# A sigmoid attention with two gated layers on one core: scores split in every batch, weights cut into 3 KB places, and a plan that is remade six times

## The chip, the core and the metric

The kernel runs on one core of a Trainium2 chip. Its engines are TensorE (PE), whose weight loads the trace shows apart as PEld, VectorE (DVE), ScalarE (ACT), GpSimd (POOL) and SyncE (SP). SP issues most of the DMAs and POOL the rest. The metric is the device time of one execution in microseconds (us), as the median of several runs.

## The reference

Three parts follow each other, all in float32:

```python
# attention: 4 batches, 12 heads, 448 tokens, head size 64
scores = q @ k^T / 8 - log(448)
x = sigmoid(scores) @ v                  # then [1792 tokens, 768]
# first layer, 768 -> 1536 -> 768
xn = x / sqrt(mean(x*x) + 1e-6) * rms_g
y = (silu(xn @ w_gate) * (xn @ w_val)) @ w_out
# second layer, 768 -> 2048 -> 768
h = y @ w_in
out = (h - tanh(h)) @ w_out2
```

## The kernel before

**Numbers in two parts.** A large product is made with three fp32r matmuls in place of one fp32 matmul. Each operand is cut into a high part (a cast to fp32r) and a low part (the value less its high part), and PE adds high·high, high·low and low·high. Each cut costs a cast on ACT or DVE and a subtraction on DVE. A call of `copy` records a cast, so all casts and copies have line 291. The subtractions have line 374 (weights), 730 and 785 (right-hand operands) and 579 (q and k).

**Attention.** A batch has six pairs of heads, and a pair lies on 128 partitions. For each pair the scores come in two halves of two 128-row pieces, ACT turns each piece into a sigmoid (line 623), and then the product with v follows (line 646). The scores of a pair are either whole fp32 matmuls (line 616) or split into three fp32r matmuls (line 596). `SPLIT_QK = (0, 1)` and `is_split` choose: pair (0, 0) and all of batches 2 and 3 are whole, the other 11 pairs are split. While attention runs, weights of the first layer are read, cut, and written back to DRAM, and from batch 2 on the right-hand operands of the first layer are made as well.

**The layers.** Batches go in two groups, (0, 1) and (2, 3). Each product uses seven block products in place of eight, whose sums and differences DVE makes. A job of a layer's first matrix (`seven_units`) has 63 matmuls (line 982), a set of its second matrix (`set_units`) 126 (line 925), and a set in the plain form (`block`) 144 (line 1007). Results of the second matrix are added up in DRAM by accumulating DMAs of POOL (line 799).

**Places.** `wt` has 8 places of 6 KB for each partition. Raw weights as they come from DRAM (`raw`), q and k of a pair (`qkr`), both parts of a job's weights (`op`), and both parts of a set's weight (`whl`, at most 3) share them. `cv` has 8 places of 3 KB, for values in float32, for weights that are read again (`again`, at most 4), and for v. `unit` has 72 places of 448 columns for all else.

**The plan.** The code records steps. `Plan.issue` then lays them out on five engine clocks with costs written in the code, and takes at each turn, of all that can start within `SOON = 300` of the soonest, the step with the lowest rank. A rank is the place in the recording plus a few offsets. The steps are then issued in order of their planned start. All engines run their own instructions in that order and wait on semaphores for each other.

Of the kernel before, what the change touches and what calls it, by code (L numbers as in the profile page):

```python
# [33 lines left out]
SPLIT_QK = (0, 1)  # L34
# [3 lines left out]
SOON = 300  # L38
# [11 lines left out]
N_UNIT, N_MOE, N_RAW, N_WT, N_CV = 72, 40, 2, 8, 8  # L50
# [21 lines left out]
class Plan:  # L72
# [21 lines left out]
    def issue(self):  # L94
        work, n_work = self.work, len(self.work)
# [12 lines left out]
        users = [[] for _ in work]  # L108
# [6 lines left out]
        slots = [list(dict.fromkeys(s for s, _ in (*w[2], *w[3]))) for w in work]  # L115
# [7 lines left out]
        free = {pool: [0.0] * size for pool, (size, _) in self.room.items()}  # L123
# [13 lines left out]
        issued = []  # L137
        frees = []
        import bisect
        import heapq  # L140

        def places(n):
# [13 lines left out]
            for k, x in want.items():  # L156
                if held[k] + x > cap[k]:
                    return None
                f = free[pool_of[k]]
                if len(f) < x:  # L160
                    return None
                t = max(t, f[x - 1])
            return t

        while len(issued) < n_work:
# [24 lines left out]
            if not cands:  # L190
                raise RuntimeError(f"no work can start; the oldest is {oldest}")
            soonest = min(c[1] for c in cands) + SOON
            finish, start, n, e, ns, uses_port = min((c for c in cands if c[1] <= soonest), key=lambda c: self.rank[c[2]])
# [3 lines left out]
            end[n], where[n], done[n] = finish + work[n][5], e, True  # L197
            waiting.remove(n)
            for s in slots[n]:
# [3 lines left out]
                if s.kind:  # L203
                    kind_at[s.kind] += 1
                    held[s.kind] += 1
                    since[s] = free[pool_of[s.kind]].pop(0)
            for s in slots[n]:
                left[s] = left.get(s, len(s.uses)) - 1
                if s.kind and not left[s]:
                    held[s.kind] -= 1  # L210
                    bisect.insort(free[pool_of[s.kind]], max(end[u] for u in s.uses) + self.OTHER)
# [6 lines left out]
            issued.append((start, n, e))  # L218
        for _, n, e in sorted(issued):
            for s in slots[n]:  # L220
                s.tile = s.tile or s.make()
            work[n][1](e)
        return max(clock.values())
# [3 lines left out]
def tile_sigmoid_attention_moe_moe(  # L227
# [20 lines left out]
    wt_p = ctx.enter_context(tc.tile_pool(name="wt", bufs=N_WT))  # L248
    cv_p = ctx.enter_context(tc.tile_pool(name="cv", bufs=N_CV))
# [5 lines left out]
        "unit": (N_UNIT, {"moe": N_MOE, "s": 18, "acc": 6, "accs": 9, "st": 4, "sum": 6, "x": 16, "xr": 4, "tmp_m": 8, "tmp_a": 4, "sq": 3, "rstd": 2,  # L255
                          "xs": 42, "tmp_s": 9, "tmp_x": 4, "qk": 12}),
        "wt": (N_WT, {"raw": N_RAW, "qkr": 4, "whl": 3, "op": 6}),
        "cv": (N_CV, {"cv": 3, "again": N_AGAIN, "vs": 3}),
# [10 lines left out]
    def unit(kind, dt=F32):  # L269
        return slot(kind, unit_p, [P, S], dt, "unit")  # L270

# [65 lines left out]
    def load_raw(src, by="SP"):  # L337
        flat = lambda t: t.bitcast(U16).rearrange("p n h -> p (n h)")
        r = slot("raw", wt_p, [P, NW + 1, 2], U32, "wt")
# [16 lines left out]
    def values32(r):  # L356


        c = slot("cv", cv_p, [P, NW], F32, "cv")
# [15 lines left out]

    def factors(j, names, of, reads):


        n = len(names)
        t = slot("op", wt_p, [P, 2, n, NH], F32R, "wt")  # L380
        w = lambda q: t.tile[:, q].rearrange("p n h -> p (n h)")
        hi, lo = (lambda: w(0), lambda: w(1)) if n == 2 else (
            lambda q=q: w(q).rearrange("p (k c) -> p k c", c=P) for q in range(2))
        split(n * NH, hi, lo, of, reads, [t["h"]], [t["l"]])
        use_factors(j, names, t)
        return t

    def use_factors(j, names, t):
        n = len(names)
        w = lambda q: t.tile[:, q].rearrange("p n h -> p (n h)")  # L390
        for x, name in enumerate(names):
            ops.setdefault(j, {})[name] = {p: (t, p, lambda k, x=x, q=q: w(q)[:, (k * n + x) * P:(k * n + x + 1) * P])
                                           for q, p in enumerate("hl")}
# [8 lines left out]
    def rows_early(ph, i):  # L402
# [15 lines left out]
        def total(to, x, y, at, sub=True):  # L418
# [3 lines left out]
            t = c[to] = c[at] if at else slot("cv", cv_p, [P, NW], F32, "cv")  # L422
# [26 lines left out]
    def pair_units(ph, i, rs, j):  # L449
# [8 lines left out]
        def sums():  # L458
            t = slot("cv", cv_p, [P, NW], F32, "cv")
# [15 lines left out]
        def keep(t, at, x):  # L475
            if (ph, i) not in SPLIT:
                put(d, at, x)
                return
            add({"SP": (2200, False)}, lambda e: nc.sync.dma_start(
                out=d.tile[:, at, :, :t.tile.shape[2] * NH], in_=t.tile.bitcast(F32).rearrange("p q n h -> p q (n h)")),  # L480
                [t["h"], t["l"]], [d[at]], after=LAND)
# [4 lines left out]
    def again(d, at):  # L486
        w = slot("again", cv_p, [P, NW], F32, "cv")
# [20 lines left out]
    def again_units(j):  # L508
        ph, _, i, _ = jobs[j]
        if (ph, i) in SPLIT:  # L510
            d = stored[ph, i]

            def load_parts(at, names):
                t = slot("op", wt_p, [P, 2, len(names), NH], F32R, "wt")
                add({"SP": (2200, False)}, lambda e: nc.sync.dma_start(
                    out=t.tile.bitcast(F32).rearrange("p q n h -> p q (n h)"), in_=d.tile[:, at, :, :len(names) * NH]), [d[at]], [t["h"], t["l"]], after=LAND)
                use_factors(j, names, t)
# [16 lines left out]
    def pair_load(b, p):  # L534
        t = qkr_t[b, p] = slot("qkr", wt_p, [P, 2 * S], F32, "wt")
# [703 lines left out]
```

## Time and profile before

| | |
|---|---|
| three runs | 1068.04 us median (1064.84, 1068.04, 1068.17) |
| the profiled execution | 1066.15 us |
| its span, first to last instruction | 1064.2 us |
| PE busy | 1042.9 us, 98% of the span |
| DVE, ACT, POOL busy | 789.2, 694.2, 141.8 us |
| moved by DMA | 245.65 MB, 231 GB/s |

The profiled execution has 2 us around its span. Matmuls overlap, so their mean duration (366 ns) says less than how far apart they start: a row such as 100 matmuls in 20.61 us does.

### The profile page before, as it was taken

Reading aid. Unit: us, or ns where it says so; the run is one execution under the profiler, and the core shown is the slowest. Engines: PE = TensorE matmul, PEld = TensorE weight load, DVE = VectorE, ACT = ScalarE, POOL = GpSimd, SP = SyncE. Lnnn points to the kernel's source line nnn. Section 1 sums busy time; section 2 is a strip of 40 time slices with the busy share of each in tenths; the row PEclk is TensorE's granted clock in tenths of the full one; section 3 lists DMA queues with packets and bytes.
Section 4 is the critical chain, followed back from the end, with each engine's and each line's share of the span. In section 5 each row is a group of like instructions: output and inputs, shape, how many; then the busy total and the mean of one; then the engine's idle time right before and its main releaser. Section 6 shows DMA issues by size and latency. Waiting matters only on the chain.

```text
span 1064.2 us, 15305 instructions
## 1 busy us (share of the span) xinstructions
PE 1042.9 (98%) x5236; PEld 880.7 (83%) x5236; DVE 789.2 (74%) x1252; ACT 694.2 (65%) x1251; POOL 141.8 (13%) x194
## 2 busy tenths in 40 slices
PE   8999999999999999999999999999999999999998
PEld 4553338999999889999998989989997899999997
DVE  3746985976877697866776668888885887777666
ACT  5776875675675566665675656777774767676752
POOL 1122001000003032101013030000303210003030
PEclk9999999999999999999999999999999999999999
DMA  6898886756759898778679399477949881839383
GB/s 202 265 309 270 252 302 219 289 179 230 274 178 244 318 258 235 266 266 322 238 247 281 116 249 304 173 253 275 240 154 258 236 241 51 282 104 236 96 192 130
DMA packets 105869, 245.65 MB, mean 231 GB/s; under 512 B 27072, under 2 KB 59328, under 8 KB 105792
## 3 DMA queue, kind: packets, MB, share of 16 engines
q1 hardware_dynamic: 82224, 179.63, 49.5%
q0 software_dynamic: 23264, 64.89, 24.8%
q8 instruction: 41, 0.67, 0.3%
q14 instruction: 36, 0.29, 0.1%
q10 hardware_dynamic: 304, 0.16, 0.1%
HBM read 151.44 MB, written 93.19 MB: 230 GB/s over the span
## 4 chain that ended last, share of the span: by engine, by line
PE 79%; issue 10%; DMA 5%; DVE 3%; POOL 2%; ACT 1%; SPq 0%; POOLq 0%; ACTq 0%; DVEq 0%
PE ps L982 39%; PE ps L925 21%; PE ps L646 7%; PE ps L1007 5%; PE ps L616 4%; PE ps L596 3%; POOL out L799 2%; DMA wt<-in_w_out 1%; DMA out<-unit 1%; DMA wt<-in_w_in 1%; DMA wt<-in_qkt 1%; DMA wAg<-cv 1%; DVE wt L374 1%; DVE unit L861 0%; DVE cv L363 0%
## 5 line engine op out<-in xcount | busy, mean ns | idle before, releaser
L982 PE MATMUL ps<-unit,wt 128*128 128x448 f32 x2520 | 522.4, 366 | 6.9 <-ACT unit L291 4.0
L982 PEld LDWEIGHTS ps<-unit,wt 128*128 128x128 f32 x2520 | 471.9, 188 | 51.0 <-ACT unit L291 6.6
L925 PE MATMUL ps<-unit,wt 128*128 128x448 f32 x1512 | 314.6, 366 | 3.5 <-DVE unit L730 1.6
L925 PEld LDWEIGHTS ps<-unit,wt 128*128 128x128 f32 x1512 | 283.4, 188 | 29.0 <-DVE unit L730 2.2
L374 DVE TENSOR_TENSOR wt<-cv,wt 128x768 fp32r<-128x768 f32 (+1 forms) x244 | 216.2, 892 | 91.1 <-ACT wt L291 88.3
L291 ACT COPY unit<-ps 128x448 f32<-128x448 f32 x297 | 156.3, 534 | 136.2 <-PE ps L982 53.6
L291 ACT CAST wt<-cv 128x768 fp32r<-128x768 f32 (+1 forms) x236 | 184.5, 786 | 81.5 <-PE ps L982 34.9
L730 DVE TENSOR_TENSOR unit<-unit 128x448 fp32r<-128x448 f32 x252 | 152.8, 620 | 36.7 <-ACT unit L291 22.1
L291 ACT CAST unit<-unit 128x448 fp32r<-128x448 f32 x259 | 143.0, 567 | 28.2 <-DVE unit L735 11.8
L861 DVE TENSOR_TENSOR unit<-ps,unit 128x448 f32<-128x448 f32 x168 | 103.4, 622 | 36.8 <-PE ps L982 19.8
L735 DVE TENSOR_TENSOR unit<-unit 128x448 f32<-128x448 f32 x144 | 87.6, 620 | 16.3 <-DMA unit<-sumB 8.9
L623 ACT ACTIVATE unit<-ps 128x448 f32<-128x448 f32 (+1 forms) x192 | 86.1, 549 | 7.3 <-PE ps L616 4.4
L646 PE MATMUL ps<-unit,cv 128*64 128x448 f32 (+1 forms) x384 | 77.5, 545 | 0.0
L799 POOL DMA_DIRECT2D sumB<-unit x48 | 41.4, 941 | 233.9 <-DVE unit L861 150.0
L363 DVE SCALAR_TENSOR_TENSOR cv<-wt,zero 128x768 uint32<-128x768 uint32 x68 | 64.8, 954 | 7.8 <-ACT zero L291 7.2
L291 ACT CAST zero<-wt 128x768 f16<-128x768 bf16 x52 | 56.0, 1076 | 11.5 <-DMA wt<-in_w_in 6.0
L1007 PE MATMUL ps<-unit,wt 128*128 128x448 f32 x288 | 60.6, 367 | 1.8 <-ACT unit L291 1.1
L646 PEld LDWEIGHTS ps<-unit,cv 128*64 128x64 f32 (+1 forms) x384 | 25.4, 136 | 44.5 <-issue 30.8
L1007 PEld LDWEIGHTS ps<-unit,wt 128*128 128x128 f32 x288 | 53.6, 188 | 7.9 <-ACT unit L291 1.8
L799 POOL DMA_DIRECT2D out<-unit x36 | 31.0, 949 | 181.6 <-DVE unit L861 165.0
L455 DVE TENSOR_TENSOR cv<-cv 128x384 f32<-128x384 f32 x80 | 42.8, 553 | 1.6 <-DMA wAg<-cv 1.0
L616 PE MATMUL ps<-wt 64*128 64x448 f32 (+1 forms) x208 | 42.7, 547 | 0.0
(49 smaller groups left out, 455.7 us busy)
## 6 DMA issues: line engine op xcount, KB each, us to landing
wt<-in_w_out POOLq DMA_DIRECT2D x28, 768.0 KB, 7.3
cv<-wD SPq DMA_DIRECT2D x56, 384.0 KB, 5.1
cv<-wB SPq DMA_DIRECT2D x36, 384.0 KB, 5.5
wt<-in_w_in SPq DMA_DIRECT2D x16, 768.0 KB, 5.9
sumB<-unit POOLq DMA_DIRECT2D x48, 224.0 KB, 8.3
wD<-cv POOLq DMA_DIRECT2D x28, 384.0 KB, 5.9
wt<-in_w_gate SPq DMA_DIRECT2D x12, 768.0 KB, 5.1
wt<-in_w_val SPq DMA_DIRECT2D x12, 768.0 KB, 5.5
```

The lines of the kernel that those rows point to most:

```text
L291: add(engines, lambda e: (nc.scalar.copy if e == "ACT" else nc.vector.tensor_copy)(to(), of()), reads, writes)
L374: add({**dve(n, psum=False), **pool(n)}, lambda e: ENG[e].tensor_sub(lo(), of(), hi().bitcast(F32)), [*reads, *kh], [*kl])
L616: nc.tensor.matmul(ps[i, c].tile[:n, :S], lhsT=t.tile[rows, at:at + n], rhs=t.tile[rows, :S], start=True, stop=True)
L623: add(act(S, psum=True), lambda e: nc.scalar.activation(to.tile[at:at + n, :S], ps.tile[:n, :S], AF.Sigmoid, bias=-math.log(S), scale=1.0 ...
L646: nc.tensor.matmul(ps.tile[i * D:(i + 1) * D, :S], lhsT=v.tile[:n, c, i, :], rhs=a[c][i].tile[:n, :], start=(c == 0), stop=(c == 3))
L730: add({**pool(S), **dve(S, psum=False)}, lambda e: ENG[e].tensor_sub(t["l"].tile, of.tile, t["h"].tile.bitcast(F32)), [of["t"], kh], [kl])
L735: add({**dve(S, psum=False), **pool(S)}, lambda e: ENG[e].tensor_sub(t.tile, x.tile, y.tile), [x["t"], y["t"]], [t["t"]])
L799: add({"POOL": (1100, False)}, lambda e: nc.gpsimd.dma_start(out=d.tile, in_=t.tile, accum_op=ALU.add), [t["t"], d["t"]], [d["t"]], after= ...
L861: add(dve(S), lambda e: nc.vector.tensor_add(t.tile, ps.tile[:, :S], t.tile), [ps["t"], t["t"]], [t["t"]])
L925: nc.tensor.matmul(ps.tile[:, :S], lhsT=part(a), rhs=x[b].tile, start=n in (1, 5) and kp == 0 and q == 0, stop=kp == n_kp - 1 and q == 2, ...
L982: nc.tensor.matmul(ps.tile[:, :S], lhsT=part(a), rhs=x[b].tile, start=n in ((1, 2, 5) if opening else (1, 5)) and i == 0 and q == 0, stop= ...
L1007: nc.tensor.matmul(ps.tile[:, :S], lhsT=wt, rhs=a[p].tile, start=start and i == 0, stop=stop and i == 2, skip_group_check=True)
```

## The change

- `SPLIT_QK` names all four batches and `WHOLE_QK = 2` leaves the first two pairs whole: 22 pairs are split in place of 11.
- The pool `wt` and the pool `cv` go. `raw` has its own two places of 6 KB; all else that was in them shares 20 places of 3 KB, called `part`. The high and low part of a weight, and q and k of a pair, are now two tiles each. At most 8 halves of `whl` (before: 3 whole ones), 8 of `op` (6 whole), 8 of `qkr` (4 whole) and 2 of `again` (4) are open at once. q and k are loaded by two DMAs in place of one, and the two parts of the jobs C 0 and C 1 are stored and loaded apart: SP issues 620 DMAs, 580 before.
- The plan is made up to six times. The first has the ranks of before; then `due` goes backward through the plan just made and gives each step the latest start that does not delay the end, and this is the rank of the next plan. The plan with the soonest modelled end is issued. `SOON` is 100.
- Caps of some kinds in `unit` grow (`accs` 12, `tmp_m` 10, `tmp_s` 12, `tmp_x` 6).

```diff
-SPLIT_QK = (0, 1)
+SPLIT_QK = (0, 1, 2, 3)
+WHOLE_QK = 2
-SOON = 300
+SOON = 100
-N_UNIT, N_MOE, N_RAW, N_WT, N_CV = 72, 40, 2, 8, 8
+PASSES = 6
+N_UNIT, N_MOE, N_RAW, N_PART = 72, 40, 2, 20
...
     def issue(self):
+        work, best, rank = self.work, None, self.rank
+        for _ in range(PASSES):
+            laid = self.lay(rank)
+            if laid is None:
+                break
+            times, freed = laid
+            ends = max(f for _, f, _ in times)
+            if best is None or ends < best[0]:
+                best = ends, times
+            rank = self.due(times, freed)
+        order = sorted((t[0], n, t[2]) for n, t in enumerate(best[1]))
...
+    def due(self, times, freed):
+        work = self.work
+        by_end = sorted(range(len(work)), key=lambda n: times[n][0])
+        end = max(f for _, f, e in times if e == "PE")
...
+        for n, us in freed.items():
+            then[n] += [(u, work[n][5] + self.OTHER) for u in us]
+        pe = [n for n in by_end if times[n][2] == "PE"]
+        for n, u in zip(pe, pe[1:]):
+            then[n].append((u, 0))
...
+            late[n] = min(-t, engine.get(e, -t)) - (f - s)
+            if e in ("PE", "DVE", "ACT"):
+                engine[e] = late[n]
...
-        "wt": (N_WT, {"raw": N_RAW, "qkr": 4, "whl": 3, "op": 6}),
-        "cv": (N_CV, {"cv": 3, "again": N_AGAIN, "vs": 3}),
+        "raw": (N_RAW, {"raw": N_RAW}),
+        "part": (N_PART, {"cv": 3, "again": 2, "vs": 3, "qkr": 8, "whl": 8, "op": 8}),
...
     def whole(j, of, reads):
-        w = whls[j] = slot("whl", wt_p, [P, 2, NW], F32R, "wt")
-        split(NW, lambda: w.tile[:, 0], lambda: w.tile[:, 1], of, reads, [w["h"]], [w["l"]])
+        w = whls[j] = {p: part_of("whl", [P, NW], F32R) for p in "hl"}
+        split(NW, lambda: w["h"].tile, lambda: w["l"].tile, of, reads, [w["h"]["t"]], [w["l"]["t"]])
...
     def is_split(b, p):
-        return b in SPLIT_QK and (b, p) != (0, 0)
+        return b in SPLIT_QK and b * HP + p >= WHOLE_QK
```

Three places in the instruction order follow. `ps` is a PSUM bank; the same lines of code have other numbers in the new file (616, 596, 646 and 982 of before are 677, 657, 707 and 1045; 623 and 839 are 684 and 902).

PE's first pairs, before:

```order
L616 MATMUL ps<-wt 128x448 x4
L616 MATMUL ps<-wt 96x448 x4
L596 MATMUL ps<-unit 128x448 x12
L646 MATMUL ps<-unit,cv 64x448 x8
L596 MATMUL ps<-unit 96x448 x12
L596 MATMUL ps<-unit 128x448 x12
```

PE's first pairs, changed:

```order
L677 MATMUL ps<-part 128x448 x4
L677 MATMUL ps<-part 96x448 x4
L677 MATMUL ps<-part 128x448 x4
L707 MATMUL ps<-unit,part 64x448 x8
L677 MATMUL ps<-part 96x448 x4
L657 MATMUL ps<-unit 128x448 x12
```

The second pair's scores now read the loaded q and k themselves; before, they read parts that DVE makes.

PE at the end of the attention, before:

```order
L616 MATMUL ps<-wt 128x448 x4
L646 MATMUL ps<-unit,cv 64x448 x8
L616 MATMUL ps<-wt 96x448 x4
L681 MATMUL ps<-ones,unit 112x1 x4
L646 MATMUL ps<-unit,cv 64x448 x8
L982 MATMUL ps<-unit,wt 128x448 x63
```

PE at the end of the attention, changed:

```order
L657 MATMUL ps<-unit 96x448 x12
L1045 MATMUL ps<-unit,part 128x448 x3
L657 MATMUL ps<-unit 128x448 x12
L707 MATMUL ps<-unit,part 64x448 x8
L1045 MATMUL ps<-unit,part 128x448 x3
L657 MATMUL ps<-unit 96x448 x12
L1045 MATMUL ps<-unit,part 128x448 x12
L657 MATMUL ps<-unit 128x448 x12
L707 MATMUL ps<-unit,part 64x448 x8
L1045 MATMUL ps<-unit,part 128x448 x6
```

The first layer's matmuls now stand between those of the last pairs: 57 of them come ahead of the last product with v, none before.

ACT at the same place, before:

```order
L623 ACTIVATE unit<-ps 96x448 x4
L291 CAST zero<-wt 128x768
L291 COPY unit<-ps 128x448
L662 ACTIVATE unit<-unit 128x448
L291 CAST zero<-wt 128x768
L291 COPY unit<-ps 128x448 x3
L839 ACT_TABLE_LOAD
L839 ACTIVATE unit<-unit 128x448 x2
```

ACT at the same place, changed:

```order
L902 ACT_TABLE_LOAD
L902 ACTIVATE unit<-unit 128x448 x2
L346 CAST zero<-raw 128x768
L684 ACT_TABLE_LOAD
L684 ACTIVATE unit<-ps 96x448 x4
L346 CAST zero<-raw 128x768
L902 ACT_TABLE_LOAD
L902 ACTIVATE unit<-unit 128x448
```

The SiLU of the first layer now comes before the last four sigmoids, so the tables change three times there; before they changed once.

## Rows read from the trace of the kernel before

**Rows 1.** The page: span, then busy time of each engine

```profile
span 1064.2 us, 15305 instructions
PE 1042.9 (98%) x5236; PEld 880.7 (83%) x5236; DVE 789.2 (74%) x1252; ACT 694.2 (65%) x1251; POOL 141.8 (13%) x194
```

**Rows 2.** Timeline of PE: start, length, work, [idle before it <- releaser]

```profile
13.00 1.65 PE L596 MATMUL ps<-unit 64*128 64x448 f32 x12 [3.19 <-DVE unit L291]
...
351.12 5.77 PE L982 MATMUL ps<-unit,wt 128*128 128x448 f32 x27 [0.72 <-ACT unit L291]
357.72 11.20 PE L982 MATMUL ps<-unit,wt 128*128 128x448 f32 x54 [0.83 <-DVE unit L861]
...
380.02 20.61 PE L1007 MATMUL ps<-unit,wt 128*128 128x448 f32 x100 [0.33 <-DVE unit L785]
...
578.37 29.50 PE L982 MATMUL ps<-unit,wt 128*128 128x448 f32 x144 [1.55 <-ACT unit L291]
...
694.49 0.67 PE L925 MATMUL ps<-unit,wt 128*128 128x448 f32 x2 [0.67 <-ACT wt L291]
...
817.97 3.95 PE L982 MATMUL ps<-unit,wt 128*128 128x448 f32 x18 [1.69 <-ACT unit L291]
...
825.87 2.09 PE L982 MATMUL ps<-unit,wt 128*128 128x448 f32 x9 [2.10 <-DVE unit L861]
...
1042.68 17.81 PE L925 MATMUL ps<-unit,wt 128*128 128x448 f32 x86 [1.31 <-DVE unit L730]
```

**Rows 3.** Chain that ended last, in the attention: start, length, work

```profile
17.81 2.60 PE ps L596 x24
20.41 3.16 PE ps L646 x16
...
105.13 3.18 PE ps L616 x16
```

**Rows 4.** Timeline of the first 14 us, three engines

```profile
6.53 3.28 PE L616 MATMUL ps<-wt 64*128 64x448 f32 x16
7.58 3.57 ACT L623 ACTIVATE unit<-ps 128x448 f32<-128x448 f32 x8 [3.70 <-PE ps L616]
...
12.46 0.39 DVE L291 CAST unit<-wt 128x448 fp32r<-128x448 f32 x1 [3.07 <-DMA wt<-in_qkt]
```

**Rows 5.** Windows in the attention's second half: stretch, length, busy PE PEld DVE ACT POOL

```profile
80.00:100.00 20.00, 20.00 (x103) 8.02 (x101) 11.13 (x22) 13.91 (x31) 4.80 (x8) 1.00 0.82 274
100.00:120.00 20.00, 20.00 (x100) 7.53 (x98) 18.66 (x34) 15.79 (x36) 2.21 (x4) 1.00 0.87 264
120.00:140.00 20.00, 20.00 (x104) 7.48 (x101) 17.67 (x33) 16.41 (x38) 1.10 (x2) 1.00 0.85 264
140.00:160.00 20.00, 20.00 (x108) 8.00 (x108) 18.05 (x30) 14.48 (x31) 0.58 (x1) 1.00 0.88 300
```

**Rows 6.** Groups by shape: work, count | busy, mean ns | idle before

```profile
L291 ACT CAST unit<-unit 128x448 fp32r<-128x448 f32 x259 | 143.0, 567 | 28.2 <-DVE unit L735 11.8 <-DVE unit L842 7.4 <-DVE unit L847 3.3
L579 DVE TENSOR_TENSOR unit<-wt,unit 128x448 fp32r<-128x448 f32 x22 | 13.8, 625 | 0.8
L839 ACT ACT_TABLE_LOAD x1 | 1.3, 1283 | 0.0
```

**Rows 7.** Timeline of ACT ahead of the stops at 351 and 578

```profile
349.62 1.06 ACT L291 CAST zero<-wt 128x768 f16<-128x768 bf16 x1 [4.67 <-DMA wt<-in_w_out]
...
576.87 1.05 ACT L291 CAST zero<-wt 128x768 f16<-128x768 bf16 x1 [4.96 <-DMA wt<-in_w_in]
```

**Rows 8.** Chain that ended last: transfers from issue to landing

```profile
335.88 13.72 DMA wt<-in_w_out
565.56 11.22 DMA wt<-in_w_in
812.12 9.70 DMA out<-unit
```

**Rows 9.** A DMA issue: count, KB each, median us to landing

```profile
cv<-wAv SPq DMA_DIRECT2D x24, 384.0 KB, 6.3
```

More of the change, by code (lines that the diff above doesn't have):

```diff
@@ L1 @@
+import bisect
+import heapq
+import itertools
 import math
@@ L107, in issue @@
                 last_write[k] = n
-        users = [[] for _ in work]
+        users = self.users = [[] for _ in work]
         for n, ds in enumerate(needs):
@@ L114, in issue @@
         end, where = [None] * n_work, [None] * n_work
-        slots = [list(dict.fromkeys(s for s, _ in (*w[2], *w[3]))) for w in work]
+        slots = self.slots = [list(dict.fromkeys(s for s, _ in (*w[2], *w[3]))) for w in work]
         taken, since = set(), {}
@@ L122, in issue @@
         kind_at = {k: 0 for k in kind_order}
-        free = {pool: [0.0] * size for pool, (size, _) in self.room.items()}
+        free = {pool: [(0.0, -1, None)] * size for pool, (size, _) in self.room.items()}
         held = {k: 0 for k in kind_order}
@@ L136, in issue @@
         oldest, done = 0, [False] * n_work
[L137 to L140, printed above, removed]
+        issued, times, freed, count = 0, [None] * n_work, {}, itertools.count()
         def places(n):
@@ L190, in issue @@
             if not cands:
-                raise RuntimeError(f"no work can start; the oldest is {oldest}")
+                return None
             soonest = min(c[1] for c in cands) + SOON
-            finish, start, n, e, ns, uses_port = min((c for c in cands if c[1] <= soonest), key=lambda c: self.rank[c[2]])
+            finish, start, n, e, ns, uses_port = min((c for c in cands if c[1] <= soonest), key=lambda c: rank[c[2]])
             clock[e] = finish
@@ L197, in issue @@
             end[n], where[n], done[n] = finish + work[n][5], e, True
+            times[n] = start, finish, e
             waiting.remove(n)
@@ L205, in issue @@
                     held[s.kind] += 1
-                    since[s] = free[pool_of[s.kind]].pop(0)
+                    since[s], _, old = free[pool_of[s.kind]].pop(0)
+                    for u in old.uses if old else ():
+                        freed.setdefault(u, []).append(n)
             for s in slots[n]:
@@ L210, in issue @@
                     held[s.kind] -= 1
-                    bisect.insort(free[pool_of[s.kind]], max(end[u] for u in s.uses) + self.OTHER)
+                    bisect.insort(free[pool_of[s.kind]], (max(end[u] for u in s.uses) + self.OTHER, next(count), s))
             if work[n][4]:
@@ L217, in issue @@
                     bisect.insort(waiting, u)
[L218 to L223, printed above, removed]
+            issued += 1
+        return times, freed
 @with_exitstack
@@ L270, in unit, with part_of @@
         return slot(kind, unit_p, [P, S], dt, "unit")
+    def part_of(kind, shape, dt=F32):
+        return slot(kind, part_p, shape, dt, "part")
     def chunk(kind="moe"):
@@ L538, in pair_load @@
         end = S + 3 * P if b < PAIRED else 2 * S
-        for e, lo, hi in (("SP", 0, S + P), ("ACT", S + P, end)) if first else (("SP", 0, end),):
-            add({e: (650, False)}, lambda e, lo=lo, hi=hi: ENG[e].dma_start(out=t.tile[:, lo:hi], in_=both[:, lo:hi]),
-                [], [t[lo // (S + P)]], after=2000)
+        for e, t, key, lo, hi in (("SP", tq, 0, 0, S), *([("SP", tk, 0, 0, P), ("ACT", tk, 1, P, end - S)] if first else [("SP", tk, 0, 0, end - S)])):
+            at = 0 if t is tq else S
+            add({e: (400, False)}, lambda e, t=t, at=at, lo=lo, hi=hi: ENG[e].dma_start(out=t.tile[:, lo:hi], in_=both[:, at + lo:at + hi]),
+                [], [t[key]], after=2000)
         if b < PAIRED:
@@ L545, in pair_load @@
                 add({"ACT" if first else "SP": (650, False)}, lambda e, rows=rows, at=at: ENG[e].dma_start(
-                    out=t.tile[rows, S + 3 * P:], in_=both[rows, at:at + D]), [], [t[2 + i]], after=2000)
-        v = vs_t[b, p] = slot("vs", cv_p, [P, 6, 2, D], F32, "cv")
+                    out=tk.tile[rows, 3 * P:], in_=both[rows, at:at + D]), [], [tk[2 + i]], after=2000)
+        v = vs_t[b, p] = part_of("vs", [P, 6, 2, D])
         def part(keys, out, of):
@@ L759, in feed @@
         f[name] = t
-        plan.later = FEED if ph in "BD" else 0
+        ends = i == {"B": KF1, "D": KF2}[ph] // 2 - 1
+        plan.later, by = FEED if ends else FEED, plan.copies_by
+        plan.copies_by = None if ends else by
         if name != "B12":
@@ L766, in feed @@
                 right_split(ph, bs, name, i, f[name])
-        plan.later = 0
+        plan.later, plan.copies_by = 0, by
     xg = {}
```

116 lines of the change are left out of this document (73 added, 43 removed).

## The prediction, as it was made before the changed kernel ran

> **What bounds the kernel now.** I read the page first: PE is busy 1042.9 of 1064.2 us, DVE 789.2 and ACT 694.2 [rows 1]. So the span is PE's own work plus 21.3 us in which PE stands still. A change gains by giving PE less to do, or by taking from those 21.3 us. The chain that ended last says the same: it runs through PE nearly everywhere, and its pieces in the attention give the price of each kind of matmul [rows 3]. PE's timeline shows where it stops [rows 2]. It waits 3.19 us for the second pair's split, and its last matmul ends at 1042.68 + 17.81 = 1060.5, which leaves 3.7 us for the last result to go out. That leaves 14.4 us for the first moments and the layers, and the seven largest stops of the layers make 8.9 of them (0.72, 0.83, 1.55, 0.67, 1.69, 2.10, 1.31) [rows 2]. Between stops the matmuls of the layers follow each other at 20.61 / 100 = 0.206 us [rows 2], which the change does not touch: their number and shapes are the same in both programs.
>
> **Scores split in 11 more pairs.** A whole pair's scores take PE 3.18 us, a split pair's 2.60; the product with v takes 3.16 in both [rows 3]. That is 0.58 us for each pair. Before, 11 pairs are split; now pairs 2 to 23 are, which is 22. PE loses 11 x 0.58 = 6.4 us of work. A page would give more: the Trainium skill, "FP8 and Floating Point Precision", section TensorE Precision Notes, says that true fp32 takes four passes, so three passes would cost 3.18 x 3/4 = 2.39 and the 11 pairs would save 8.7 us. The measured 2.60 decides, and I keep 6.4.
>
> The price lies on DVE and ACT. Each split pair adds two subtractions of 0.625 us on DVE [rows 6], 22 x 0.625 = 13.8 us, and two casts. I counted in the built program that the casts go to ACT: up to the last product with v, ACT has 35 casts of 448 columns in place of 12, DVE 30 in place of 31. So ACT gets 23 x 0.567 = 13.0 us [rows 6]. Besides, ACT now changes its table three times at the end of the attention, before once: 2 x 1.28 = 2.6 us more [rows 6]. The Trainium skill, "ScalarE: Activation LUTs", section What ACT_TABLE_LOAD costs, speaks against this order: it counts a drain with each switch, 2.66 us together, and wants functions batched by table set. By that the two switches cost 5.3 us of ACT, not 2.6; the row before shows no idle time ahead of the load, so I use 2.6.
>
> Is there room? From 80 to 160 us, where the 11 pairs lie, DVE is busy 11.1 + 18.7 + 17.7 + 18.1 = 65.5 us and ACT 60.6 [rows 5]. With the additions, DVE has 79.3 and ACT 76.2, while the stretch shrinks from 80 to 73.6. That would not fit. But 57 matmuls of the first layer now stand among the last pairs, 57 x 0.206 = 11.7 us. They are taken from later, so they lengthen nothing, and they cover PE while DVE works: 73.6 + 11.7 = 85.3 us for 79.3 of DVE. That is 93% full, and DVE seldom runs so densely for long, since it waits for ACT's casts. From below the crowding costs 0; from above it gives the whole gain of the scores back, 6.4. I take 2, nearer to nothing, because in the built program each part of q and k stands at least 13 of the attention's matmuls ahead of its use.
>
> **The second pair whole.** PE's stop at 13.00 is a wait for DVE's casts, and DVE waited 3.07 us for the load [rows 2, 4]. Now the second pair needs no split, and SP's order has its q and k as third and fourth DMA, ahead of all v; only two small pieces come later, for the last piece of the scores. What is late next? The first pair ends at 6.53 + 3.28 = 9.81 and fills all eight banks. ACT empties the first four by about 7.58 + 3.57 / 2 = 9.4, so the second pair's first half can start at once and takes 1.6 us. The product with v needs all eight sigmoids, at 11.15 [rows 4], when PE is still busy. I take 2.9 of the 3.19 us. The bounds are 0 (the load is as late as before) and 3.2. That this pair is now 0.58 us dearer is already in the count of 11.
>
> **Places and the new ranks in the layers.** Two things move here. First, weights stand further ahead of PE. A set's weight was one of three; now its halves are eight places. Counted in matmuls between the subtraction that ends a weight and the first matmul that reads it: before, 0 in the nearest of 84 cases, 12 cases below 8 matmuls (1.6 us), the median 29; now the nearest is 20 and the median 54. That meets the stops at 694 (0.67, weights late) and 1042 (1.31). Raw weights no longer wait for a place that PE must give back, as the load ahead of 351 did; a larger pool meets 351, 357 and 578 (3.1 together) in part. The stops at 818 and 826 (3.8) I leave as they are: there the places of `unit` come back late from accumulating DMAs, 9.70 us from issue to landing [rows 8], and `unit` has still 72 places and the same DMAs. So 0.67 + 1.31 + 3.1 = 5.1 us are within reach, and I take 3. From below, all of the layers' stops could go (about 11); from above there could be new ones, which is the rival below.
>
> Second, loads stand nearer to their use. Weights that are read again had a median of 95 matmuls (19.6 us) from the DMA's issue to its first reader in the program's order, and now 41 (8.4 us); 77 of 164 lie below 40, before 7. The slowest kind of these lands after 6.3 us in the median [rows 9], so it is still hidden, with less to spare. 40 more DMAs (24 for q and k, 16 for the jobs C) cost only issue time on SP, which waits most of the time.
>
> **The sum.** Against the profiled execution, 1066.15: -6.4 (scores), +2 (crowding), -2.9 (start), -3 (stops) = -10.3, which gives 1055.9, in round numbers 1056. The median of the three runs lies 1.9 above the profiled execution, which the range covers.
>
> **Rivals.**
> - *All stops of the layers go and nothing crowds.* The plan is made for that. Then -6.4 - 2.9 - 10 = 1047. Against it: some of the stops come from transfers that land after 10 to 14 us [rows 8], which no order of steps foresees.
> - *The attention becomes bound by DVE.* The 57 matmuls are not ready in time, and DVE's 79.3 us set the stretch. The gain of the scores goes back: 1066.15 - 2.9 - 3 + 1 = 1061 to 1062. For it: 93% is dense. Against it: from 80 to 100 DVE is busy for 11.1 of 20 us only [rows 5], so there is room to start earlier.
> - *Loads come too late, slower than before.* Place: weights read again and raw weights, 164 + 68 loads. When one is late, ACT, which works in order, stands at its cast. Rows show the price: transfers of 13.72 and 11.22 us held ACT for 4.67 and 4.96 us and cost PE 0.72 + 0.83 and 1.55, thus 1.55 each [rows 2, 7, 8]. With half the distance and half the places for `again`, such a load happens more often. My gain of 10.3 is used up by 10.3 / 1.55 = 7 more of them, and from 9 on the kernel is measurably slower. With 14 of 232 it takes 1055.9 + 21.7 = 1078. Against it: a place in a pool of 20 is often free before the plan says, and SP then issues earlier; and ACT's work on weights has got 20 matmuls or more to spare.
>
> **How the numbers follow.** Forecast (1050 to 1062 by its own): 0.48. All stops gone, 1047: 0.14. DVE bound, 1062: 0.22. Late loads, 1078: 0.16. A measurement of this kernel tells about 0.3% from no change, 3.2 us, so faster means below 1064.8 and slower above 1071.2. Faster: 0.48 + 0.14 + 0.16 of the third = 0.78. Same: 0.06 of the third and 0.03 of the fourth = 0.09. Slower: 0.13. The range of 1047 to 1068 leaves out about half of the second case and most of the fourth, some 0.2.
>
> **What would show it.** Right: a profile in which PE is busy about 6 us less, pair after pair takes 2.60 + 3.16 us also from 80 us on, PE's first stop after the first scores is below 0.5 us, no stop of PE stands behind a weight's subtraction, and the stops at the accumulating DMAs are still there. Wrong: PE standing between the last pairs with DVE as the releaser (the second rival), ACT's casts with idle time ahead of them released by DMAs in many places of the layers (the third), or scores of a split pair in batches 2 and 3 that take PE more than 2.60 us.

## The result, and the profile after

The changed kernel takes 1076.07 us (median of five runs, 1072.33 to 1076.45). The kernel before, run beside it, takes 1064.84. The ratio of the means is 1.0087, with a 95% interval of 1.0059 to 1.0115; the medians lie 11.2 us apart. So it is slower, by 9 us, where I had forecast 10 us faster; it is also above the range of 1047 to 1068.

The page of the profiled execution (1072.33 us):

```profile
span 1070.6 us, 15552 instructions
PE 1042.7 (97%) x5324; PEld 891.9 (83%) x5324; DVE 794.1 (74%) x1282; ACT 693.5 (65%) x1267; POOL 141.2 (13%) x194
```

PE is as busy as before [rows 1], though 6.4 us of its work are gone. The rest of the span, in which PE stands, is 27.9 us, before 21.3. PE's timeline (start, length, stop ahead of it) shows where:

```profile
33.08 4.92 PE L707 MATMUL ps<-unit,part 128*64 128x448 f32 x16 [3.50 <-ACT unit L684]
50.23 1.15 PE L657 MATMUL ps<-unit 64*128 64x448 f32 x5 [4.24 <-DVE unit L346]
138.19 0.92 PE L742 MATMUL ps<-ones,unit 128*112 128x1 f32 x8 [1.29 <-DVE unit L730]
...
346.95 5.72 PE L1045 MATMUL ps<-unit,part 128*128 128x448 f32 x27 [1.48 <-ACT unit L346]
353.64 23.93 PE L1045 MATMUL ps<-unit,part 128*128 128x448 f32 x117 [0.97 <-DVE unit L924]
...
519.07 39.42 PE L1045 MATMUL ps<-unit,part 128*128 128x448 f32 x180 [4.51 <-DVE unit L924]
...
827.22 7.55 PE L1045 MATMUL ps<-unit,part 128*128 128x448 f32 x36 [1.62 <-ACT ps L346]
```

The stops at 13, 694 and 1042 us [rows 2] are gone, as forecast. The longest new ones are those at 33, 50, 138 and 519. Behind each of the four PE runs at half its clock. The windows around them (busy times of PE, PEld, DVE, ACT, POOL, then the granted clock, DMA share, GB/s) show it, and the stretch that [rows 5] cut in four stands below them:

```profile
30.00:40.00 10.00, 6.92 (x36) 3.33 (x38) 7.44 (x12) 6.43 (x15) 2.17 (x4) 0.83 0.67 203
48.00:56.00 8.00, 5.77 (x23) 2.13 (x25) 6.59 (x13) 4.08 (x10) 0.55 (x1) 0.79 0.51 148
136.00:146.00 10.00, 8.71 (x54) 4.79 (x52) 9.61 (x17) 5.79 (x14) 0.00 (x0) 0.83 0.73 243
516.00:528.00 12.00, 8.93 (x31) 8.07 (x32) 9.46 (x17) 5.34 (x10) 0.00 (x0) 0.72 0.76 274
80.00:160.00 80.00, 78.69 (x514) 42.57 (x512) 66.42 (x121) 64.88 (x144) 11.33 (x18) 0.98 0.84 269
```

A window of 10 us with a mean clock of 0.83 has 10 x (1 - 0.83) x 2 = 3.4 us at the lower level, 1.2 GHz. The four windows have 3.4 + 3.4 + 3.4 + 6.7 = 17 us of it. Before, the windows of the same parts stood at 1.00. The chain that ended last shows the price on one piece, and that the split scores do cost what they should in batches 2 and 3:

```profile
28.81 2.73 DMA part<-in_qkt
33.08 4.97 PE ps L707 x16
38.28 9.32 DMA part<-in_qkt
...
51.38 4.50 PE ps L707 x16
...
92.64 2.60 PE ps L657 x24
95.25 3.16 PE ps L707 x16
```

A product with v takes 3.16 us, but 4.97 and 4.50 behind the first two stops.

What PE waited for at 33 and 50 us stands in the timeline of SP, POOL, ACT and DVE:

```profile
31.56 0.56 ACT L346 CAST unit<-part 128x448 fp32r<-128x448 f32 x1 [3.99 <-DMA part<-in_qkt]
32.51 3.54 ACT L684 ACTIVATE unit<-ps 96x448 f32<-96x448 f32 x8
...
37.44 1.07 POOL L395 DMA_DIRECT2D raw<-in_w_out  x2
38.28 0.54 SPq L601 DMA_DIRECT2D part<-in_qkt  x1
...
43.47 5.69 SPq L611 DMA_DIRECT2D part<-in_vp  x4
47.62 0.39 DVE L346 CAST unit<-part 128x448 fp32r<-128x448 f32 x1 [7.78 <-DMA part<-in_qkt]
```

ACT works in order: its cast of a q stands for 3.99 us in front of eight sigmoids that are ready, and PE needs these. That q is the seventh pair's, while PE is at the product of the fourth; it landed 2.73 us after its issue, little more than the 2.4 that the plan counts (0.4 to issue, 2.0 to land). So what is late here is the issue, and the cast that ACT has in front of ready work is one for a pair that PE does not need yet. DVE stands 7.78 us for a q that was issued at 38.28 and landed 9.32 us later, behind two raw weights of 768 KB that POOL had issued at 37.44. From 43.47 on SP stands as well: eight of its DMAs are out by then, and it issues the next one at 47.62, when the oldest of them (38.28 + 9.32 = 47.60) has landed. The other two stops have the same form with a raw weight, here that at 519:

```profile
503.75 0.33 SPq L395 DMA_DIRECT2D raw<-in_w_in  x1
...
515.38 1.05 ACT L346 CAST zero<-raw 128x768 f16<-128x768 bf16 x1 [5.43 <-DMA raw<-in_w_in]
...
516.46 0.96 DVE L418 SCALAR_TENSOR_TENSOR part<-raw,zero 128x768 uint32<-128x768 uint32 x1 [5.42 <-ACT zero L346]
517.33 0.62 DVE L924 TENSOR_TENSOR unit<-ps,unit 128x448 f32<-128x448 f32 x1
```

The raw weight is waited for 11.6 us after its issue; behind ACT's cast stands DVE's step on the same weight, and behind that the additions that free PE's banks. At 138 PE waits for DVE's L730, and DVE had stood 3.40 us for a raw weight that was issued at 130.23:

```profile
130.23 0.45 SPq L395 DMA_DIRECT2D raw<-in_w_gate  x1
...
136.39 0.61 DVE L346 CAST zero<-raw 128x768 f16<-128x768 bf16 x1 [3.40 <-DMA raw<-in_w_gate]
...
137.42 0.62 DVE L730 TENSOR_TENSOR unit<-unit 128x448 f32<-128x448 f32 x1
```

Over the whole kernel the loads of q and k (L601) and those of raw weights (L395) land after:

```profile
DMA to landing us min/median/max: 2.4/3.2/10.2
DMA to landing us min/median/max: 4.2/7.1/12.7
```

Loads landed as late before. There a load of q and k behind two raw weights took 9.6 us (both issues, and its landing), and PE did not stop:

```profile
36.27 1.12 POOL L340 DMA_DIRECT2D wt<-in_w_out  x2
...
38.30 0.76 SPq L540 DMA_DIRECT2D wt<-in_qkt  x1
DMA to landing us min/median/max: 9.6/9.6/9.6
```

What changed is how far the loads are ahead. SP has issued 42 DMAs by 28.7 us in both kernels. Before, they held q and k of seven pairs; now, with one DMA more for each pair, of six. And PE itself is 2.4 us further, for its stop at 13 us is gone. The scores behind the third pair's product, before and changed:

```profile
29.26 2.67 PE L596 MATMUL ps<-unit 64*96 64x448 f32 x24
```

```profile
26.90 2.68 PE L657 MATMUL ps<-unit 64*96 64x448 f32 x24
```

My theory after this reading (L): the plan counts 2.0 us for q, k and v and 4.5 us for weights from the end of the issue, so it issues them that late, while the slow ones land after 6 to 12 us. Engines that work in order then stand, PE stops, and the half clock behind each stop adds to the price. The rivals were the new ranks (R), the denser DVE and ACT (C), and more DMA pieces on SP (P). For the stops at 50 and 519 L has its rows (9.3 and 11.6 us); L does not fit the other two as well: the load behind the stop at 33 landed in 2.7 us, and the one behind that at 138 landed after 6.1 us, within the 6.7 that the plan counts for it (2.2 to issue, 4.5 to land).

### The profile page after: what moved, and what is told of

Read it like the earlier page. It is cut to its first block, busy times and chain, and to the rows that moved or that the text cites. A ratio compares the mean times of both kernels' runs of the same rounds, so it can differ in the third digit from the quotient of the medians.

```text
span 1070.6 us, 15552 instructions
## 1 busy us (share of the span) xinstructions
PE 1042.7 (97%) x5324; PEld 891.9 (83%) x5324; DVE 794.1 (74%) x1282; ACT 693.5 (65%) x1267; POOL 141.2 (13%) x194
## 4 chain that ended last, share of the span: by engine, by line
PE 81%; DMA 7%; issue 5%; DVE 3%; SPq 2%; ACT 1%; POOL 1%; POOLq 0%; DVEq 0%; ACTq 0%
PE ps L1045 41%; PE ps L988 24%; PE ps L707 6%; PE ps L1070 5%; PE ps L657 4%; DMA part<-in_qkt 1%; DMA part<-wB 1%; POOL out L862 1%; DMA raw<-in_w_in 1%; DMA part<-wAg 1%; SPq L611 1%; DMA out<-unit 1%; DMA part<-in_vp 1%; DMA part<-in_vt 1%; DVE part L429 1%
## 5 line engine op out<-in xcount | busy, mean ns | idle before, releaser
L1045 PE MATMUL ps<-unit,part 128*128 128x448 f32 x2520 | 525.4, 366 | 10.7 <-DVE unit L924 7.1
L1045 PEld LDWEIGHTS ps<-unit,part 128*128 128x128 f32 x2520 | 473.2, 188 | 57.2 <-DVE unit L924 9.0
L988 PE MATMUL ps<-unit,part 128*128 128x448 f32 x1512 | 311.4, 364 | 0.0
L988 PEld LDWEIGHTS ps<-unit,part 128*128 128x128 f32 x1512 | 283.5, 187 | 22.3
L429 DVE TENSOR_TENSOR part<-part 128x768 fp32r<-128x768 f32 (+1 forms) x244 | 215.7, 891 | 69.5 <-ACT part L346 66.9
L346 ACT CAST part<-part 128x768 fp32r<-128x768 f32 (+1 forms) x236 | 182.4, 786 | 12.4 <-DMA part<-wB 4.7
L707 PE MATMUL ps<-unit,part 128*64 128x448 f32 (+1 forms) x384 | 82.3, 568 | 3.5 <-ACT unit L684 3.5
L418 DVE SCALAR_TENSOR_TENSOR part<-raw,zero 128x768 uint32<-128x768 uint32 x68 | 64.9, 954 | 23.7 <-ACT zero L346 23.4
L346 ACT CAST zero<-raw 128x768 f16<-128x768 bf16 x52 | 56.0, 1077 | 23.7 <-DMA raw<-in_w_in 12.6
L657 PEld LDWEIGHTS ps<-unit 64*128 64x128 f32 (+1 forms) x528 | 45.3, 173 | 26.3 <-issue 13.9
L657 PE MATMUL ps<-unit 64*128 64x448 f32 (+1 forms) x528 | 62.7, 378 | 4.2 <-DVE unit L346 4.2
L707 PEld LDWEIGHTS ps<-unit,part 128*64 128x64 f32 (+1 forms) x384 | 26.5, 142 | 47.6 <-issue 32.0
L1070 PE MATMUL ps<-unit,part 128*128 128x448 f32 x288 | 60.3, 365 | 1.9 <-DVE unit L848 1.0
L1070 PEld LDWEIGHTS ps<-unit,part 128*128 128x128 f32 x288 | 53.7, 188 | 7.5 <-DVE unit L848 1.7
```

Of the source, the lines that this page charges most:

```text
L346: add(engines, lambda e: (nc.scalar.copy if e == "ACT" else nc.vector.tensor_copy)(to(), of()), reads, writes)
L429: add({**dve(n, psum=False), **pool(n)}, lambda e: ENG[e].tensor_sub(lo(), of(), hi().bitcast(F32)), [*reads, *kh], [*kl])
L657: nc.tensor.matmul(ps[i, c].tile[:n, :S], lhsT=parts[w].tile[rows, at:at + n], rhs=parts[x].tile[rows, :S], start=q == 0, stop=q == 2)
L707: nc.tensor.matmul(ps.tile[i * D:(i + 1) * D, :S], lhsT=v.tile[:n, c, i, :], rhs=a[c][i].tile[:n, :], start=(c == 0), stop=(c == 3))
L988: nc.tensor.matmul(ps.tile[:, :S], lhsT=part(a), rhs=x[b].tile, start=n in (1, 5) and kp == 0 and q == 0, stop=kp == n_kp - 1 and q == 2, ...
L1045: nc.tensor.matmul(ps.tile[:, :S], lhsT=part(a), rhs=x[b].tile, start=n in ((1, 2, 5) if opening else (1, 5)) and i == 0 and q == 0, stop= ...
```

## Experiments

Each was timed against the kernel before on the same chip (its median there 1066.4 to 1066.9). Stops are PE's, in profiled executions.

**Which part of the change costs?** Three kernels take it apart.

*One pass of the plan (changed kernel).*

```diff
-PASSES = 6
+PASSES = 1
```

> The changed kernel with one pass of the plan (ranks in the recorded order, as before), all else as changed. Theory R (the new ranks move loads too close to their use): the stops of PE of 3.50, 4.24 and 4.51 us go, PE's granted clock is above 0.997, and the kernel takes 1060 to 1068. Theory L (the loads' modelled landing, 2.0 us for q, k and v, is too short whatever the ranks are; with it stand the two places for weights that are read again): stops over 3 us behind late q or k stay, at least one stretch of half clock follows them, and the kernel takes 1070 to 1085. Theory C (the 11 more split pairs crowd DVE and ACT): 1070 or more, with stops between 80 and 160 us.

1075.26 us, 1.0069 (1.0046 to 1.0092). Stops of 4.42 (59 us), 2.69, 2.68 and 2.15 us, four stretches of half clock. R falls: without the new ranks the loss is nearly the same. C is not excluded: a stop of 1.61 us at 134, with half clock behind it, lies in the stretch that it names.

*Split scores alone (kernel before).*

```diff
-SPLIT_QK = (0, 1)
+SPLIT_QK = (0, 1, 2, 3)
```

> The kernel before with the scores of batches 2 and 3 split too, nothing else (pools, ranks and the second pair as before). Theory R: no stop of 3 us after the first 20 us, clock 0.999, 1066.15 - 6.4 + 0 to 3 = 1060 to 1063. Theory L: the q and k loads of batches 2 and 3 are now read by casts, which need them earlier, at the same modelled 2.0 us: one or two stops over 1 us between 80 and 160, 1060 to 1066. Theory C: stops of PE between 80 and 160 us that DVE or ACT releases, 5 us or more in sum, and 1066 or more.

1067.15 us, 1.0006 (0.9991 to 1.0021). The 6.4 us don't arrive. Stops of 0.45, 1.51 and 0.93 us lie between 119 and 130 us, with half clock behind them; their sum of 2.9 lies between what L and C expected. (The profile is of an execution of 1072.02 us, with half clock at the start besides.)

*Pools and ranks without the further split (changed kernel).*

```diff
-SPLIT_QK = (0, 1, 2, 3)
-WHOLE_QK = 2
+SPLIT_QK = (0, 1)
+WHOLE_QK = 1
```

> The changed kernel with the scores as before (11 split pairs, the first pair whole): pools, pieces of q and k and ranks as changed. If the pools and the additional DMAs of q and k make the loads late: stops over 2 us at casts between 20 and 70 us and half clock behind them, and 6.4 us more of scores than the changed kernel: 1074 to 1084. If the 11 more split pairs bring the loss: no stop over 2 us before 150 us, 1060 to 1066.

1070.29 us, 1.0036 (1.0023 to 1.0048), between the two expectations: a stop of 4.92 at 60 us behind a cast, with half clock, and stops of 2.52 and 3.11 in the layers. So pools and ranks alone cost 3.7 us, and the split, which should take 6.4 us off, adds another 5.4 (by the ratios).

**Are the modelled landing times the cause?**

*q, k and v at 7.0 us (changed kernel; three places).*

```diff
-after=2000
+after=2000 if (b, p) == (0, 0) else 7000
```

> The changed kernel with 7.0 us in place of 2.0 as the plan's landing time of q, k and v (but for the first pair), ranks and pools as changed. Theory L: the stops at 33, 50 and 138 us and the three stretches of half clock behind them go (3.5 + 4.2 + 1.3 of stops, 10.2 us at half clock = 5.1), the stop at 519 with its 6.8 us of half clock stays: 1072.3 - 14 = 1058 to 1063. Theory R: the ranks still hold loads back; at least two of the three stops stay, 1068 to 1074. Rival P (SP is bound by issuing more pieces at the start, 4.5 us for each pair): the stops at 33 and 50 stay, since SP can't issue earlier, and only that at 138 goes: 1070 to 1072.

1066.35 us, 0.9990 (0.9973 to 1.0008): 10 us better, though above what L expected and below R and P. The stop at 33 is gone; near 138 there are 0.89 and 0.67, near 50 still 2.15 and 0.97, and 1.88 and 2.80 at 506 and 514. P does not fall. SP issues no earlier: the seventh pair's q goes out at 28.76 (28.81 in the changed kernel), as its 43rd DMA in both. What moved is the reader, for ACT now has the eight sigmoids ahead of its next cast:

```profile
28.76 0.58 SPq L601 DMA_DIRECT2D part<-in_qkt  x1
```

```profile
29.61 3.54 ACT L684 ACTIVATE unit<-ps 96x448 f32<-96x448 f32 x8
33.11 0.57 ACT L346 CAST unit<-part 128x448 fp32r<-128x448 f32 x1
```

So at this stop the longer landing time helps because the plan no longer puts the cast of a load that isn't there in front of work that is ready. A kernel with q and k in one DMA, which would test P, was not run. The 12 runs of this kernel lie between 1061.06 (mean clock 0.998) and 1071.06 (0.992).

*All loads at 7.0 us.* In addition to the last, for raw weights by SP and for weights that are read again:

```diff
-after=LAND
+after=7000
```

> As the last, and the plan's landing time of raw weights issued by SP and of weights that are read again is 7.0 us in place of 4.5 as well. Theory L: besides, the stop at 519 (4.51 us, 6.8 us of half clock behind it) and those at 347 and 354 (2.4 us together) go: no stretch of half clock is left, clock 0.998 or more, 1050 to 1057. Theory R: no better than the last. If the longer times only push other work late: 1060 or more, with stops in other places.

1057.07 us, 0.9912 (0.9890 to 0.9933), 9.6 us below before and the fastest kernel of this study, at the upper end of what L expected. Page and PE's timeline:

```profile
span 1057.8 us, 15556 instructions
PE 1039.6 (98%) x5324; PEld 890.5 (84%) x5324; DVE 791.7 (75%) x1284; ACT 693.1 (66%) x1265; POOL 140.7 (13%) x194
```

```profile
9.15 6.47 PE L677 MATMUL ps<-part 64*128 64x448 f32 x24 [1.92 <-DMA part<-in_qkt]
...
72.52 5.88 PE L707 MATMUL ps<-unit,part 128*64 128x448 f32 x16 [2.88 <-DMA part<-in_vp]
145.17 0.47 PE L1045 MATMUL ps<-unit,part 128*128 128x448 f32 x1 [2.27 <-DVE part L429]
...
771.32 11.18 PE L1045 MATMUL ps<-unit,part 128*128 128x448 f32 x54 [1.11 <-DVE unit L924]
824.43 2.08 PE L1045 MATMUL ps<-unit,part 128*128 128x448 f32 x9 [1.51 <-DVE unit L924]
```

The stops behind 330 us are 4.8 in sum (before 12.2, changed 12.3). Up to 150 us three long ones are left, all behind loads, with half clock behind all three (the product with v behind the second takes 5.88). L had expected no half clock; the profiled execution has a mean clock of 0.993, the others 0.995 to 0.998.

*The same, and one pass.*

```diff
-PASSES = 6
+PASSES = 1
```

> The kernel with 7.0 us for all these loads (1057.07), with one pass of the plan. If the ranks are worth nothing: 1055 to 1059. If they pay once the landing times are right: 1061 to 1070, with more and longer stops of PE in the layers. If they cost: below 1054.

1064.83 us, 0.9990 (0.9978 to 1.0003). So between these two plans the six passes are worth 7.8 us; with the short landing times they were worth nothing. The table of neighbours below shows that two plans can lie as far apart for other reasons.

*All loads at 7.0 us, without the further split.*

```diff
-SPLIT_QK = (0, 1, 2, 3)
-WHOLE_QK = 2
+SPLIT_QK = (0, 1)
+WHOLE_QK = 1
```

> The kernel with 7.0 us for all these loads, with the scores as before (11 split pairs, the first pair whole). If the 11 more split pairs are worth their 6.4 us once loads come in time: 1062 to 1065. If they crowd DVE and ACT and so give some of it back: 1057 to 1061.

1062.95 us, 0.9968 (0.9949 to 0.9988); four of its 12 runs have a clock of 1.000. So between these two plans the further split is worth 5.9 us, near the 6.4 of its work.

*The kernel before with split scores and 7.0 us.* In the kernel before:

```diff
-SPLIT_QK = (0, 1)
+SPLIT_QK = (0, 1, 2, 3)
...
-after=2000
+after=2000 if (b, p) == (0, 0) else 7000
...
-after=LAND
+after=7000
```

> The kernel before with the scores of batches 2 and 3 split, and 7.0 us in place of 2.0 for q, k and v and in place of 4.5 for raw weights and weights that are read again. Pools, ranks and the first two pairs as before. Theory L (the missing 6.4 us of the run with split scores alone went to late loads): the stops of 0.45, 1.51 and 0.93 us between 119 and 130 us go, with the half clock behind them, 1057 to 1061. Theory C (11 more split pairs crowd DVE and ACT there, whenever the loads land): these stops stay, 1064 to 1068. Rival (8 places of 6 KB can't hold loads that are issued earlier): stops at places that come free late, 1068 or more.

1068.08 us, 1.0013 (0.9999 to 1.0026). The stops of 1.50 and 0.93 us at 122 stay. In the old places L is not enough: C holds for this spot, or something in those pools that I did not single out. With the new pools and six passes the spot is free; with one pass and all loads at 7.0 us, stops of 0.51 and 1.62 us stand near it (123 and 131), so the pools alone do not free it.

**Is it the two raw loads side by side (theory D)?**

*Raw weights of POOL in turn (changed kernel).* Behind each raw load a small DMA writes `turn` in DRAM; the next raw load is recorded as a reader of it.

```diff
+    if by == "POOL":
+        add({by: (1100, False)}, lambda e: ENG[e].dma_start(out=turn_d, in_=r.tile[:, 1:5]),
+            [r["t"]], [turn["t"]], after=0)
```

> The changed kernel, with the raw w_out loads of POOL one after the other: a small DMA that reads the raw weight stands between two of them in POOL's queue, so the second is issued only when the first has landed (the plan counts 5.0 us for one in place of 9.0). q, k and v keep 2.0 us. Theory D (two raw loads of 768 KB side by side make the DMAs of SP behind them land after 8 to 10 us, and SP stands when 8 of its DMAs are out): the DMAs of SP issued just behind a raw load land within 7 us, the stops at 33 and 50 us shrink below 1.5 us each, and with the half clock behind them the kernel gains 3.5 + 4.2 + 3.4 - 3 = 8: 1065 to 1070. Rival L (the same bytes land in the same time, only the lead of a load counts): the stops stay over 3 us, 1072 to 1080.

1071.86 us, 1.0055 (1.0034 to 1.0076). The stops near 33 and 50 us shrink to 1.64, 1.16 and 0.85, but a stop of 3.73 comes at 146, and 2.57, 2.27 and 1.97 in the layers. Behind one raw weight, q (37.88) lands after 7.2 us in place of 9.3, as D says of this spot; but the time is above D's range and just below its rival's, and the kernel gains 4 us of the 8.

*The same with all loads at 7.0 us.* The edits of raw weights in turn and of all loads, with POOL's raw loads at 5.0:

```diff
-after=LAND if by == "SP" else 2 * LAND
+after=7000 if by == "SP" else 5000
```

> The kernel with 7.0 us for all these loads, and POOL's raw w_out loads one after the other. The stops of 1.92, 2.88 and 2.27 us that were left at 9, 73 and 145 us and 8 us of half clock behind them (4 us of time) followed raw loads that landed together. Theory D: the first two go, 1048 to 1055. Rival L (total bytes count, not their neighbours): 1056 to 1062.

1068.92 us, 1.0022 (0.9999 to 1.0046). Worse than with the loads side by side, and above both expectations: the start has a stop of 4.09. Loads in turn did not make a better kernel.

*A plan that shares one path between transfers (changed kernel).* The core of the edit, in `lay`; each DMA is recorded with its size `kb`:

```diff
+    if self.kb[n] and len(landed[e]) >= 8:
+        r = max(r, landed[e][-8])
...
+    moved = max(moved, start + 1000) + self.kb[n] / 400 * 1000
+    landed[e].append(max(moved + 1500, finish + work[n][5]))
```

> The changed kernel with a plan that lets transfers share one path: each lands at the later of its issue + 1.0 us and the end of the transfers before it, plus its size at 400 KB a us, plus 1.5 us, and SP and POOL may have 8 DMAs out each. Theory D: the plan now knows where loads land late, so the stops over 2 us go: 1050 to 1060. Rival L (a load needs a constant reserve, because its landing varies more than such a sum can say): loads stand as near to their use as before, half clock stays in three or four places, 1064 to 1076.

1086.97 us, 1.0198 (1.0169 to 1.0227), the slowest. Its timeline around the longest stop, and the window:

```profile
138.03 0.60 DVE L355 CAST zero<-raw 128x768 f16<-128x768 bf16 x1 [5.92 <-DMA raw<-in_w_gate]
...
142.97 0.74 PE L666 MATMUL ps<-unit 64*128 64x448 f32 x1 [5.80 <-DVE unit L355]
```

```profile
140.00:152.00 12.00, 8.74 (x32) 3.70 (x34) 9.24 (x18) 7.41 (x17) 0.00 (x0) 0.57 0.69 226
```

That is above both expectations, so neither D nor its rival had it right. The edit also replaces all constants and SP's issue costs (0.6 us for a load), so the runs do not show which part of it is at fault. The constants, of the change or of 7.0 us, are better than this model.

**Landing times, or the luck of one plan (rival N)?** Every constant makes another order. Five more variants of the two numbers (q, k and v; weights), against 2.0 and 4.5 of the change and 7.0 and 7.0. The edits are those of all loads with other numbers, here the first:

```diff
-after=2000
+after=2000 if (b, p) == (0, 0) else 9000
...
-after=LAND
+after=7000
```

9.0 and 7.0: 

> The kernel with 7.0 us for raw weights and for weights that are read again, and 9.0 in place of 7.0 us for q, k and v. If the reserve of q, k and v was still too short (stop of 2.88 behind v at 73 us): that stop goes with the 8 us of half clock behind it, 1050 to 1055. If the rest is due to transfers that no constant covers: 1056 to 1061.

1.5 and 4.5: 

> The changed kernel with 1.5 us in place of 2.0 for q, k and v, 4.5 for the weights as it was. Theory L (short landing times make the loads late): 1070 to 1082, two stops or more over 2.5 us, clock 0.993 or less. Rival N (a plan's time varies by 5 us or more whatever the landing times are, and 1057 was luck): anywhere from 1055 to 1080.

2.0 and 4.3: 

> The changed kernel with 4.3 us in place of 4.5 for raw weights and weights that are read again, q, k and v at 2.0 as they were. Theory L: 1068 to 1082, clock 0.994 or less. Rival N: anywhere from 1055 to 1080.

6.0 and 7.0: 

> The changed kernel with 6.0 us for q, k and v and 7.0 for raw weights and weights that are read again. Theory L: 1055 to 1063, as with 7.0 for all (1057.07) and with 9.0 and 7.0 (1062.26). Rival N: anywhere from 1055 to 1080.

8.0 and 7.0: 

> The changed kernel with 8.0 us for q, k and v and 7.0 for raw weights and weights that are read again. Theory L: 1055 to 1063. Rival N: anywhere from 1055 to 1080.

| q, k, v | weights | us | ratio | longest stop near 50 us |
|---|---|---|---|---|
| 2.0 | 4.5 (the change) | 1076.07 | 1.0087 | 4.24 |
| 1.5 | 4.5 | 1071.97 | 1.0052 (1.0036 to 1.0068) | 5.19 |
| 2.0 | 4.3 | 1072.19 | 1.0056 (1.0038 to 1.0075) | 6.25 |
| 6.0 | 7.0 | 1068.56 | 1.0020 (1.0001 to 1.0039) | 2.78 |
| 7.0 | 7.0 | 1057.07 | 0.9912 | none over 0.2 |
| 8.0 | 7.0 | 1059.64 | 0.9930 (0.9903 to 0.9958) | 2.74 |
| 9.0 | 7.0 | 1062.26 | 0.9954 (0.9938 to 0.9971) | 2.65 |

The three plans with short times and the four with long ones don't overlap, which speaks for the landing times as a cause. But within the long ones 11 us lie between 6.0 and 7.0, so one plan's luck (N) is as large: 1057 is the best of several draws, and the four have a mean of 1062. The two short settings came out as L expected; L missed at 6.0 (over 1063), and 9.0 came out above both of its ranges: the stop at 73 is gone, but others of 2.65 and 1.99 came at 57 and 118. With so few draws the size of the effect stays open, and so does why the stop near 50 us, behind two raw weights issued at 34 us, is still there in three of the four.

## Why the prediction was wrong

The account of the profiled executions, 1064.2 to 1070.6:

| term | forecast | measured |
|---|---|---|
| scores | -6.4 | -6.4 of work; in time, 5.9 between two plans |
| attention's stops (start -2.9, crowding +2) | -0.9 | +6.6 (5.1 to 11.7 before 330 us) |
| layers' stops | -3 | +0.1 (12.2 to 12.3) |
| half clock | not in the sum | +6.2 |

The last is PE's busy time against its work: 1042.7 - (1042.9 - 6.4). A part of it is the execution compared with: that of before had a mean clock of 0.999, where others of the same kernel had 0.994 to 1.000.

- *Scores.* Right. Pairs of batches 2 and 3 take 2.60; the estimate from the four passes of the Trainium skill, "FP8 and Floating Point Precision", section TensorE Precision Notes, would have made it 2.39, which no pair shows.
- *Crowding.* No sign of it: DVE is busy 66.4 of 80 us, before 65.5, as its work moved away from there. ACT's two further table loads take 1.28 each with no idle time ahead. The stop at 138 has DVE as its releaser, the sign of the second rival, but DVE had stood for a raw weight, not worked. The second rival did not happen.
- *The second pair whole.* The stop of 3.19 went, as said. What was late next I had sought in the first pairs alone. SP issues without a pause from 14 to 38 us, and PE first stopped behind the load whose cast began at 31.56.
- *Stops of the layers.* The mechanism was right: 694 and 1042 are gone, and with all loads at 7.0 us the layers lose 7.4 us of stops, more than my 3. (My list of the seven largest had missed one of 0.93 at 835.) In the changed kernel one late raw weight at 519 (4.51) took it back.
- *The step that failed* is the loads, which my sum put at nothing: "it is still hidden, with less to spare", and "40 more DMAs ... cost only issue time on SP, which waits most of the time". From 14 to 38 us SP does not wait, and with its further pieces q and k are a pair behind (six pairs by 28.7 us, before seven) while PE is 2.4 us ahead, and the stops of 3.50 and 4.24 stand behind two of these loads. The other two, 1.29 and 4.51, stand behind raw weights, whose distance to their reader I had not looked at. For weights that are read again I compared the distance with the median landing in the kernel before [rows 9], while those to be feared land last: the median of raw `in_w_in` is 7.7 us now, and the one issued at 503.75 was waited for 11.6. The engines that stand for them work in order, and SP never had more than eight DMAs out. With that the attention's stops measured +6.6 in place of -0.9. The half clock behind them, +6.2, had no term at all.
- *The price.* My third rival, late loads, is what happened, with a chance of only 0.16. Its place was wrong in part: two of the four stops hang on a q, the other two on raw weights, and none on a weight that is read again. Its price of 1.55 us per late load was far too small. A stop cost its length and, four times here, half clock behind it. [Rows 2] held no sign of the second, for in that execution no stop was followed by it.

## What to carry to other kernels

In a plan that issues loads as late as its model lets it, take the landing time from the slow end of what the trace shows under load (here 7 us was better than 2), look whether the issuing engine can issue as early as the plan says, and read for each load what stands in order behind its first reader. Price a stop of TensorE with the half clock that may follow, and read the granted clock of before and after for the same stretches. A planner's constants should be tried with their neighbours, since here two neighbours lay 11 us apart, as much as the change was to gain.

## What the runs showed of the hardware

A stop of PE in the attention of 1.3 us (138.19) already was followed by 3.4 us at 1.2 GHz. It is no fixed rule: the stops of 1.48 and 0.97 at 347 and 354 in the same execution were followed by none (granted clock 1.00 from 347 to 360), and the stop near 13 us, nearly the same in the kernel before and in the one with split scores alone, was followed by half clock in only one of the two profiled executions. Before ([rows 2], 13.00):

```profile
12.00:20.00 8.00, 7.00 (x50) 4.04 (x52) 4.17 (x9) 3.94 (x9) 0.00 (x0) 1.00 0.56 161
```

Split scores alone, PE's timeline and the same window:

```profile
13.13 2.61 PE L596 MATMUL ps<-unit 64*128 64x448 f32 x12 [2.94 <-DVE unit L291]
```

```profile
12.00:20.00 8.00, 6.87 (x26) 3.44 (x28) 3.77 (x8) 1.96 (x4) 0.00 (x0) 0.57 0.56 166
```

In the same 8 us PE gets through 26 recorded matmuls, before 50. Runs of one kernel differ by it: those of the kernel before have mean clocks of 0.994 to 1.000. The Trainium skill, "TensorE: Matmul & The Clock Gate", section HAM oscillation — how this bites in real kernels, tells of a kernel whose PE comes back at half clock after each wait for a transfer, so that the wait costs more than its length. The rows at 33 and 50 us agree: a stop of 3.50 and one of 4.24, and behind them 4.97 and 4.50 in place of 3.16.

Small loads behind large ones land behind them. Behind two raw weights of 768 KB (37.44) a q of 224 KB took 9.32 us, where the same kind took 2.73 at 28.81, and what SP issued in the meantime, pieces of 16 KB too, landed after it.
